# Retention and GELU MLP on one core: block 1's state, scores and outputs moved forward, masks built later

## The chip, the cores and the metric

The kernel runs on 1 core of one Trainium2 chip. The metric is the device time of one execution in microseconds (us). Before the change it is 288.76 us, the median of 3 runs (288.71 to 288.97).

In the profile the engines are PE (TensorE, matrix products), PEld (its weight loads), DVE (VectorE), ACT (ScalarE), POOL (GpSimd) and SP (SyncE, which here only issues DMA transfers; its queue is shown as SPq). L419 is line 419 of the kernel before.

## The reference

Retention over 8 batches and 8 heads, 576 positions, head size 64, then a two-layer MLP with a tanh GELU over the 4608 tokens.

```python
def _attn_ref(q, k, v):
    scores = scale * np.matmul(q, k.transpose(0, 1, 3, 2))
    gamma = 1.0 - 2.0 ** (-5.0 - np.arange(H, dtype=np.float32))
    rel = pos[:, None] - pos[None, :]
    Dmat = np.where(rel >= 0, gamma[:, None, None] ** rel[None, :, :], 0.0)
    return np.matmul(scores * Dmat[None, :, :, :], v)

def _moe_ref(x, w_in, w_out):          # x: 4608 x 512, d_ff: 2048
    h = x @ w_in
    g = 0.5 * h * (1.0 + np.tanh(c * (h + 0.044715 * h * h * h)))
    return g @ w_out
```

All inputs and the output are float32.

## The kernel before

The retention is done in chunks. Each batch has four chunks of 128 positions and a tail of 64; the tails of all batches make a ninth block of tokens. Within a chunk, scores are masked and multiplied with the values; what came before a chunk enters through a state (keys times values), which is carried from half chunk to half chunk by a decay. So a batch b goes through these steps, each of them a helper:

- `load` and `cc` (cast): the chunks of k, q and v come in as float32 by DMA issued on SP, into a ring of 16 buffers (`ld`). POOL, ACT or DVE casts them to float16 and scales k and q by powers of the decay (L294 for k, L275 for q, L271 on POOL or L269 on ACT for v). `pump` issues the next load for each buffer that a cast frees.
- `turn_dma` (L324): two DMA transposes on SP bring the cast k and q into `tt`, with the head dimension on partitions. Batches 0 and 1 are turned by PE instead.
- `scores`: 64 matmuls of 64x64 (L419, `st <- tt`) into four PSUM banks, then `masks` (L444, DVE): four multiplications with the causal mask `cm`, which give `ret` and release the banks. `masks(b, 0)` handles the first two chunks and `masks(b, 1)` the last two.
- `state` (L419, `us <- cv, ck`): 32 matmuls of 64x64 for two chunks, into two PSUM banks. `scan_halves` on DVE (L494, L477, L472) adds them up with the decay `gx` and, between the operations, has ACT cast the running state to float16 (L497); `spread` casts the state behind the chunk (L505). `later(b, c)` is a scan and a spread.
- `outs(b, g)`: first the contributions of the states to two chunks (`xs <- tt, tbb`), then, between two tiny matmuls called `turn`, the `state` of what comes next, then the contributions of the states that are read from the other half of the partitions and of the masked scores (`xs <- ret, cv`); about 90 to 98 small matmuls with the state among them. `put` then casts `xs` into `xT`, the MLP's input, on ACT (one of them on DVE).

The MLP works on blocks of 512 tokens (t = 0 to 8). Layer one multiplies xT with w_in, and ACT applies the GELU into `gT` (L605 and L612 in halves for t = 0 and 1, L584 and L590 for the others). `act_sums` (L746 to L750, DVE) forms sums of gT for a seven-product scheme, by which layer two (`prod`, L769) needs seven block products of 256 columns instead of eight; `after` adds the products up on DVE and ACT (L783, L822, L839) and stores them in two halves, `send` (L786), by DMA on SP.

The order of all work is written out by hand. Block t is a list of steps, numbered 0 to 29 here: 0 to 15 are layer one (in block 1 eight matmuls of 256 columns each, from block 2 on four matmuls of 512 columns for each), 16 to 29 the fourteen pieces of layer two (m, u) in the order m = 1, 6, 5, 7, 2, 4, 3, eight matmuls each. `at(t, u, f)` puts the retention work f of the next batch behind step u of block t, and `run` calls it there. Every engine executes its instructions in that order, and waits only for what it reads or for a buffer that it overwrites. So block 1 computes batch 1's MLP while batch 2's retention is prepared, and block t prepares batch t + 1.

The eight PSUM banks are handed out by `bank` from a queue, the longest released first, and given back by `drop`.

Around the change, in block 1 before:

- step 0: POOL builds the masks `cm` and `tm` (`chunk_masks`, L218 and L220) and the decays `gx` (`decays_turned`, L232), between its casts of batch 1 and those of batch 2.
- end of block 0: `after(0, 4, ...)` issues the store of the second half of block 0's output on SP, behind the loads of batch 2's values up to there.
- steps 0 to 10: the casts of batch 2, and at step 5 its two transposes on SP.
- step 12: the loads of batch 3 may be issued (`resume`); step 16: POOL waits at `gate` (L1077), a copy of one column of the last sum of gT, before it casts batch 3.
- step 16: `state(2, 0)`; steps 17 and 18: `later(2, 0)` and `later(2, 1)`; step 19: `scores(2)` with both masks; step 25: `outs(2, 0)` with `state(2, 1)`, and `later(2, 2)`; step 26: `later(2, 3)`; step 28: `outs(2, 1)` with `state(3, 0)`.

In the blocks 2, 3 and 4 the scores of the next batch stand behind step 10, in the later ones behind step 9.

Of the kernel before, what the change touches and what calls it, by code (L numbers as in the profile page):

```python
# [20 lines left out]
def kernel(  # L21
# [9 lines left out]
    nc = tc.nc  # L31
# [19 lines left out]
    gam = [1.0 - 2.0 ** (-5.0 - h) for h in range(H)]  # L51
# [129 lines left out]
    for n in range(2):  # L181
# [3 lines left out]
            out=lp[:, 32 + 16 * n : 48 + 16 * n].rearrange("p (x h) -> p x h", h=8),  # L185
# [12 lines left out]
    tbb = [const.tile([128, 2 * NC - 1, HP, 64], F16, name=f"tbb{i}") for i in range(2)]  # L198
# [17 lines left out]
    def chunk_masks():  # L216
        for m, pattern in ((cm, [[1, 2], [2, 32]]), (tm, [[1, 64]])):
            nc.gpsimd.memset(m, 1.0)  # L218
            for r, base in ((128, 64), (64, 0)):
                nc.gpsimd.affine_select(  # L220
                    out=m[0:r], in_=m[0:r], compare_op=ALU.is_ge, fill=0.0, base=base, pattern=pattern, channel_multiplier=-1
                )
# [6 lines left out]
    def decays_turned():  # L229
        for h in range(H):  # L230
            u = 64 * (h % 2 ^ h // 4)
            nc.gpsimd.memset(gx[u : u + 64, h // 2, :], gam[h] ** 128)  # L232

    tbt = [const.tile([128, HP, 64], F16, name=f"tbt{i}") for i in range(NT4)]

# [204 lines left out]
    def masks(b, g):  # L440
        n = 8 if b < PAIR else 4
        for r, t in enumerate(att[b].pop(("st", g))):
            m = sb.tile([128, 512], F16, tag="ret", name="ret", bufs=6)
            nc.vector.tensor_tensor(  # L444
                out=m[:, 0 : 64 * n].rearrange("p (n i) -> p n i", n=n), in0=t[:, 0 : 64 * n].rearrange("p (n i) -> p n i", n=n),
                in1=(cm if b < PAIR else tm).unsqueeze(1).to_broadcast([128, n, 64]), op=ALU.mult,
            )
            drop(t)
            att[b]["ret"][g, r] = m
# [35 lines left out]
        if last:  # L485
            drop(us)

    def scan_halves(b, c):
        a = att[b]
        us, o = a.pop(("U", c))  # L490
        u, v = (t[:, 256 * o : 256 * o + 256].rearrange("p (q d) -> p q d", d=64) for t in us)
        if c == 0:
            t = sb.tile([128, HP, 64], F32, tag="ts", name="ts", bufs=2)
            nc.vector.tensor_copy(out=t, in_=u)  # L494
        else:
            t = plus(u, a["w"], "ts")
        nc.scalar.copy(out=tbb[b % 2][:, 2 * c], in_=t)  # L497
        times(a, c, plus(v, t, "vs"), gx)
        if o == 1:
            drop(us[0]), drop(us[1])  # L500
# [275 lines left out]
    def after(t, m, u):  # L776
        last = t == NTB - 1
        if u == 0 and not (last and m == 3 or t in WIN and m == 4) or u == 1 and t in WIN and m == 4:
            return
        def pr(tag):  # L780
            return op[tag].rearrange("p (u d) -> p u d", u=2)
        def add(o, a, b):
            nc.vector.tensor_tensor(out=o, in0=a, in1=b, op=ALU.add)  # L783
        def send(o, i):
            if t < B:
                nc.sync.dma_start(  # L786
                    out=out[S * t : S * t + TB, :].rearrange("(u i p) d -> p u i d", u=2, i=2)[:, :, i, :], in_=o
                )
                return
            both(o, i, slice(0, HD))  # L790
        def both(o, i, d):
            rows = out.rearrange("(b s) d -> b s d", s=S)
            for h, e in enumerate((nc.sync, nc.scalar)):
                r = rows[2 * i + h :: 4, M0 : M0 + TL, d]
                e.dma_start(out=r.rearrange("v s d -> s v d"), in_=o[TL * h : TL * h + TL, :, d])
        def end(o, i, v, d=slice(0, DM)):
            b = 4 * v + 2 * i
            for h, e in enumerate((nc.sync, nc.scalar)):
                r0 = S * (b + h) + M0
                e.dma_start(out=out[r0 : r0 + TL, d], in_=o[TL * h : TL * h + TL, d])  # L800
        if t == 0 and m != 1 and m != 2:
            if m == 6:
                for n, a, b in (("u2", "s1", "B"), ("u3", "u2", "C")):
                    keep[n] = sb.tile([128, 2, HD], F32, tag="k" + n[1], name="k" + n[1], bufs=1)
                    add(keep[n], keep[a], pr(b))
                    drop(op.pop(b))
                add(keep["o0"][:, :, HD:DM], keep["u3"], pr("E"))
                drop(op.pop("E"))
                send(keep["o0"], 0)
            elif m == 7:  # L810
                keep["o1"] = ost()
                add(keep["o1"][:, :, HD:DM], keep["u3"], pr("D"))
                add(keep["u2"], keep["u2"], pr("D"))
                drop(op.pop("D"))
            elif m == 4:
                add(keep["o1"][:, :, 0:HD], keep["u2"], pr("F"))
                drop(op.pop("F"))
                send(keep["o1"], 1)
            return
        if m == 1:  # L820
            keep["s1"] = sb.tile([128, 2, HD], F32, tag="k1", name="k1", bufs=1)
            nc.scalar.copy(out=keep["s1"], in_=pr("A"))  # L822
        elif m == 6:
            keep["u2"] = sb.tile([128, 2, HD], F32, tag="k2", name="k2", bufs=1)
            add(keep["u2"], keep["s1"], pr("B"))
            for f in range(0, NH if t in WIN else 0, 2):
                act_sums(t, f, f + 2, parts=(1,))
        elif m == 7:
            keep["u3"] = sb.tile([128, 2, HD], F32, tag="k3", name="k3", bufs=1)
            add(keep["u3"], keep["s1"], pr("B"))  # L830
            keep["o1"] = ost()
            add(keep["o1"][:, :, HD:DM], keep["u3"], pr("C"))
            if last:
                both(keep["o1"], 1, slice(HD, DM))
            drop(op.pop("B")) if t in WIN else None
            drop(op.pop("C")) if t in WIN else None
        elif m == 2:
            keep["o0"] = ost()
            nc.scalar.copy(out=keep["o0"][:, :, 0:HD], in_=pr("A"))  # L839
            drop(op.pop("A"))  # L840
            if last:
                both(keep["o0"], 0, slice(0, HD))
        elif m == 5 and t in WIN:
            add(keep["u2"], keep["u2"], pr("C"))
        elif m == 3 and last:
            add(keep["o0"][:, u, HD:DM], keep["u2"][:, u], pr("EF"[u])[:, u])
            end(keep["o0"][:, u], 0, u, slice(HD, DM))
        elif m == 3:
            x = "E" if t in WIN else "C"
            add(keep["o0"][:, :, HD:DM], keep["u2"], pr(x))  # L850
            drop(op.pop(x))
            send(keep["o0"], 0)
        elif m == 4 and t in WIN:
            add(keep["o1"][:, :, 0:HD], keep["u3"], pr("D"))
            drop(op.pop("D"))
            send(keep["o1"], 1)
        elif m == 4:
            add(keep["o1"][:, :, 0:HD], keep["s1"], pr("B"))
            drop(op.pop("B"))
            send(keep["o1"], 1)  # L860
# [27 lines left out]
    def later(b, c):  # L888
        (scan if b < NPE else scan_halves)(b, c)
        spread(b, c, A.copy)  # L890
# [53 lines left out]
    def at(t, u, f, last=False):  # L944
        events.setdefault((t, u, last), []).append(f)
# [60 lines left out]
    group(1, 0, ((0, 8), (0, 10)), (0, 10), (0, 12), late=(1, 1))  # L1006
    casts2(1, 1, (0, 10), (0, 10), P)
    group(1, 1, ((0, 13), (1, 0)), (1, 2), (1, 5), late=(1, 6))
    at(1, 0, lambda: (chunk_masks(), decays_turned()))

    at(6, 0, lambda: load_tails(TP[7]))
    at(6, 18, lambda: cast_tails(TP[7]))
# [5 lines left out]
    for t, b in TP.items():  # L1018
        at(t, 3, lambda b=b: tail_values(b))

    def scores(b, tails=None):
        w = [score(b, g) for g in range(2)] if b < B else []
        if tails is not None:
            w.append(score(PAIR + tails, 0))
        pack(w)
        if b < B:
            masks(b, 0), masks(b, 1)
        if tails is not None:
            masks(PAIR + tails, 0)

# [13 lines left out]
        for x in todo:  # L1044
            put(*x)

    U2 = (19, 25, 28)
    at(1, 16, lambda: pack([state(2, 0)]))
    for c in range(2):
        at(1, 17 + c, lambda c=c: later(2, c))  # L1050
    for t in range(1, B):
        b, tl = t + 1, TP.get(t)
        s0, o0, o1 = U2 if t == 1 else (10 if t in (2, 3, 4) else 9, 15, 24)
        at(t, s0, lambda b=b, tl=tl: scores(b, tl))
        at(t, o0, lambda b=b, tl=tl: outs(b, 0, tl, (b, 1) if b < B else None))
        if b == B:
            continue
        at(t, 25 if t == 1 else 16, lambda b=b: later(b, 2))
        at(t, 26 if t == 1 else 20, lambda b=b: later(b, 3))
        at(t, o1, lambda b=b: outs(b, 1, None, (b + 1, 0) if b + 1 < B else None))  # L1060
        if b + 1 < B:
            for c in range(2):
                at(t + 1, c, lambda c=c, nb=b + 1: later(nb, c))
# [119 lines left out]
```

## Time and profile before

| what | value |
| --- | --- |
| median of 3 runs | 288.76 us (288.71 to 288.97) |
| the profiled execution, its own time | 288.71 us |
| its span in the profile | 287.0 us |
| granted TensorE clock over the span | 1.0 |
| HBM read, written | 36.70 MB, 9.44 MB |
| L584 PE MATMUL, 352 of 128x512 | 79.0 us busy, 379 ns mean |
| L605 PE MATMUL, 256 of 128x256 | 29.9 us busy, 273 ns mean |
| block 1, layer one | 51.1 to 67.8 us |
| block 1, layer two | 67.8 to 84.7 us |
| blocks 2, 3, 4 | 84.7 to 114.0, to 143.4, to 172.8 us |

The time of one execution is a little longer than the span, which runs from the first to the last recorded instruction. Busy time on PE counts each matmul from its start to its modelled end, and neighbours overlap; a mean of 273 ns for 256 columns does not mean that one starts every 273 ns (they start 109 ns apart). A number in brackets behind an instruction of the timeline is the engine's idle time before it, and the name behind the arrow what ended it; "issue" is written where the profile shows nothing that the engine waited for. In a line of stretches each engine has its busy time and the count of its instructions, then come the granted clock, the share of time in which the 16 DMA engines were busy, and GB/s.

### The profile page before, as it was taken

Reading aid. Unit: us, or ns where it says so; the run is one execution under the profiler, and the core shown is the slowest. Engines: PE = TensorE matmul, PEld = TensorE weight load, DVE = VectorE, ACT = ScalarE, POOL = GpSimd, SP = SyncE. Lnnn points to the kernel's source line nnn. Section 1 sums busy time; section 2 is a strip of 40 time slices with the busy share of each in tenths; the row PEclk is TensorE's granted clock in tenths of the full one; section 3 lists DMA queues with packets and bytes.
Section 4 is the critical chain, followed back from the end, with each engine's and each line's share of the span. In section 5 each row is a group of like instructions: output and inputs, shape, how many; then the busy total and the mean of one; then the engine's idle time right before and its main releaser. Section 6 shows DMA issues by size and latency. Waiting matters only on the chain.

```text
span 287.0 us, 9420 instructions
## 1 busy us (share of the span) xinstructions
PE 274.5 (96%) x3986; PEld 202.1 (70%) x3986; DVE 196.5 (68%) x412; ACT 169.3 (59%) x326; POOL 115.3 (40%) x225
## 2 busy tenths in 40 slices
PE   6889998999989999999999999999999999999993
PEld 3558876888864588458844884488448887887782
DVE  6785988686866664577368636763687767875863
ACT  5477655996248563866386746574666358407800
POOL 5579859980692089007910670059230000000000
PEclk9999999999999999999999999999999999999999
DMA  7999999989989999999799859997972030012013
GB/s 200 304 380 339 386 295 260 254 217 188 234 186 221 247 218 182 248 226 230 167 218 267 203 127 241 243 225 126 254 162 39 2 148 1 2 47 103 0 39 110
DMA packets 127306, 54.09 MB, mean 188 GB/s; under 512 B 93472, under 2 KB 119072, under 8 KB 127264
## 3 DMA queue, kind: packets, MB, share of 16 engines
q1 hardware_dynamic: 126672, 52.97, 76.5%
q8 instruction: 31, 0.51, 0.8%
q10 hardware_dynamic: 592, 0.52, 0.6%
q14 instruction: 11, 0.09, 0.1%
HBM read 36.70 MB, written 9.44 MB: 161 GB/s over the span
## 4 chain that ended last, share of the span: by engine, by line
PE 81%; DMA 9%; DVE 3%; POOL 3%; issue 1%; ACT 1%; SPq 0%; POOLq 0%; DVEq 0%
PE hp L584 26%; PE opB L769 13%; PE opA L769 10%; PE opC L769 9%; PE hp L605 5%; DMA ld<-in_moe_w_in_dram 4%; PE hB L678 3%; PE xs L419 3%; DMA ld<-in_q_dram 3%; DMA ld<-in_moe_w_out_dram 2%; PE hC L678 2%; PE st L419 2%; POOL cq L283 1%; PE us L419 1%; PE opD L769 1%; PE tr L312 1%
## 5 line engine op out<-in xcount | busy, mean ns | idle before, releaser
L584 PE MATMUL hp<-xT,w_in_sb 128*128 128x512 f16 x352 | 79.0, 379 | 0.0
L590 ACT ACTIVATE gT<-hp 128x512 f16<-128x512 f32 x88 | 50.8, 598 | 29.6 <-PE hp L584 29.1
L769 PEld LDWEIGHTS <-gT 128*128 128x128 f16 x576 | 55.0, 98 | 8.7 <-issue 1.2
L584 PEld LDWEIGHTS <-w_in_sb 128*128 128x128 f16 x352 | 34.0, 98 | 37.9 <-DVE xT L570 0.2
L769 PEld LDWEIGHTS <-s 128*128 128x128 f16 x432 | 42.0, 98 | 4.9
L769 PE MATMUL opA<-w_out_sb,gT 128*128 128x256 f16 x288 | 36.2, 273 | 0.7 <-ACT w_out_sb L875 0.5
L294 POOL TENSOR_TENSOR ck<-ld,sc 128x128 f16<-128x128 f32 (+1 forms) x72 | 33.5, 491 | 4.2 <-DMA ld<-in_k_dram 4.2
L746 DVE TENSOR_TENSOR s<-gT 128x512 f16<-128x512 f16 x36 | 16.1, 448 | 26.2 <-ACT gT L590 19.6
L605 PE MATMUL hp<-xT,w_in_sb 128*128 128x256 f16 x256 | 29.9, 273 | 1.1 <-POOL w_in_sb L875 0.7
L275 POOL TENSOR_TENSOR cq<-ld,sc 128x256 f16<-128x256 f32 x48 | 29.8, 639 | 0.0
L1077 POOL COPY gate<-s 128x1 f16<-128x1 f16 x5 | 0.9, 190 | 71.5 <-DVE s L750 71.5
L605 PEld LDWEIGHTS <-w_in_sb 128*128 128x128 f16 x256 | 24.3, 98 | 5.5 <-POOL w_in_sb L875 2.5
L769 PE MATMUL opB<-wt,gT 128*128 128x256 f16 x224 | 26.8, 273 | 0.0
L570 ACT CAST xT<-xs 128x512 f16<-128x512 f32 x23 | 15.4, 735 | 13.1 <-PE xs L419 13.1
L783 DVE TENSOR_TENSOR k<-k,opB 128x512 f32<-128x512 f32 x17 | 11.7, 686 | 13.4 <-PE opB L769 11.5
L612 ACT ACTIVATE gT<-hp 128x512 f16<-128x512 f32 x32 | 18.5, 603 | 3.8 <-PE hp L605 3.5
L747 DVE TENSOR_TENSOR s<-s,gT 128x512 f16<-128x512 f16 x36 | 16.8, 468 | 1.2
L769 PE MATMUL opB<-wt,s 128*128 128x256 f16 x144 | 17.4, 273 | 0.0
L769 PE MATMUL opC<-wt,s 128*128 128x256 f16 x144 | 17.2, 273 | 0.0
L748 DVE TENSOR_TENSOR gT<-gT 128x512 f16<-128x512 f16 x36 | 16.7, 463 | 0.0
L444 DVE TENSOR_TENSOR ret<-st,cm 128x512 f16<-128x512 f32 x24 | 14.9, 683 | 2.4 <-PE st L419 2.4
L750 DVE TENSOR_TENSOR s<-gT,s 128x512 f16<-128x512 f16 x36 | 16.0, 457 | 0.0
(135 smaller groups left out, 429.1 us busy)
## 6 DMA issues: line engine op xcount, KB each, us to landing
ld<-in_q_dram SPq DMA_DIRECT2D x32, 256.0 KB, 5.5
ld<-in_k_dram SPq DMA_DIRECT2D x32, 256.0 KB, 5.6
ld<-in_v_dram SPq DMA_DIRECT2D x32, 256.0 KB, 5.3
out_dram<-ost SPq DMA_DIRECT2D x16, 512.0 KB, 4.0
ld<-in_moe_w_in_dram SPq DMA_DIRECT2D x16, 256.0 KB, 5.7
ld<-in_moe_w_out_dram SPq DMA_DIRECT2D x16, 256.0 KB, 5.8
lt<-in_k_dram SPq DMA_DIRECT2D x8, 128.0 KB, 5.0
lt<-in_q_dram SPq DMA_DIRECT2D x8, 128.0 KB, 4.2
```

The costliest lines, as they stand in the source:

```text
L275: eng.tensor_tensor(out=a[key][:, 1024 * g + 512 * x : 1024 * g + 512 * x + 512].rearrange("p (n l d) -> p l n d", l=2, d=D)[:, y ^ x], in ...
L294: eng.tensor_tensor(out=dh[:, o], in0=x, in1=sc[:, s0, i].unsqueeze(2).to_broadcast(list(x.shape)), op=ALU.mult)
L419: nc.tensor.matmul(out, lhsT, rhs, start=k not in opened, stop=True, skip_group_check=True)
L584: nc.tensor.matmul(hp.rearrange("p (g t) -> p g t", t=TL), w_in_sb[:, ct, 128 * fc : 128 * fc + 128], xT[:, o : o + TB // TL, ct, :], star ...
L590: nc.scalar.activation(out=gT[t][:, fc].rearrange("p i n -> p (i n)"), in_=hp, func=AF.Gelu_apprx_tanh)
L605: nc.tensor.matmul(hps[n][:, 256 * x : 256 * x + 256].rearrange("p (g t) -> p g t", t=TL), w_in_sb[:, ct, 128 * (fs[n] + x) : 128 * (fs[n] ...
L612: nc.scalar.activation(out=gT[t][:, f : f + 2, 2 * u : 2 * u + 2, :].rearrange("p f i n -> p f (i n)"), in_=hp.rearrange("p (f n) -> p f n ...
L746: nc.vector.tensor_tensor(out=s["1"], in0=a21, in1=a22, op=ALU.add)
L747: nc.vector.tensor_tensor(out=s["2"], in0=s["1"], in1=a11, op=ALU.subtract)
L748: nc.vector.tensor_tensor(out=a21, in0=a11, in1=a21, op=ALU.subtract)
L750: nc.vector.tensor_tensor(out=s["4"], in0=a12, in1=s["2"], op=ALU.subtract)
L769: nc.tensor.matmul(op[tag][:, HD * u : HD * u + HD], lhs(f), rhs[:, f], start=(new and f == 0), stop=(f == NH - 1), skip_group_check=True,)
```

## The change

- `decays_turned` sets `gx` on DVE (`nc.vector.memset`) instead of POOL; it stays behind step 0 of block 1.
- `chunk_masks` moves from step 0 to step 11 of block 1, and so, on POOL, behind the casts of batch 2.
- The store of the second half of block 0's output is issued at step 6 of block 1. On SP it then stands behind the two transposes of batch 2 instead of ahead of them.
- `state(2, 0)` moves from step 16 to step 12, into layer one. Both its scans run behind step 14, on DVE ahead of the last `act_sums` of block 1 (`scan_halves` gets a parameter `then`, by which the cast of the running state on ACT is issued later, at steps 16 and 17). The spreads stay at 17 and 18.
- `scores(2)` moves from step 19 to 17; `masks(2, 0)` follows there, `masks(2, 1)` at step 19.
- `outs(2, 0)` moves from step 25 to 22, with `later(2, 2)` at 22 and `later(2, 3)` at 24. `outs(2, 1)` stays at 28.
- In blocks 2, 3 and 4 the scores move from step 10 to step 9.

No matmul or weight load of PE is added or removed (7,972; with branches and waits of their own the program has 7,990 PE instructions before and 7,992 after); DVE gains the eight memsets that POOL loses.

```diff
     def decays_turned():
         for h in range(H):
             u = 64 * (h % 2 ^ h // 4)
-            nc.gpsimd.memset(gx[u : u + 64, h // 2, :], gam[h] ** 128)
+            nc.vector.memset(gx[u : u + 64, h // 2, :], gam[h] ** 128)
...
-    def scan_halves(b, c):
+    def scan_halves(b, c, then=lambda f: f()):
...
-        nc.scalar.copy(out=tbb[b % 2][:, 2 * c], in_=t)
+        then(lambda: nc.scalar.copy(out=tbb[b % 2][:, 2 * c], in_=t))
         times(a, c, plus(v, t, "vs"), gx)
...
             elif m == 4:
                 add(keep["o1"][:, :, 0:HD], keep["u2"], pr("F"))
                 drop(op.pop("F"))
-                send(keep["o1"], 1)
+                at(1, 6, lambda o=keep["o1"]: send(o, 1))
...
-    at(1, 0, lambda: (chunk_masks(), decays_turned()))
+    at(1, 0, decays_turned)
+    at(1, 11, chunk_masks)
...
-    def scores(b, tails=None):
+    def scores(b, tails=None, wait=None):
...
         if b < B:
-            masks(b, 0), masks(b, 1)
+            masks(b, 0)
+            at(*wait, lambda: masks(b, 1)) if wait else masks(b, 1)
...
-    U2 = (19, 25, 28)
-    at(1, 16, lambda: pack([state(2, 0)]))
+    U2 = (17, 22, 28)
+    at(1, 12, lambda: pack([state(2, 0)]))
     for c in range(2):
-        at(1, 17 + c, lambda c=c: later(2, c))
+        at(1, 14, lambda c=c: scan_halves(2, c, lambda f, c=c: at(1, 16 + c, f)))
+        at(1, 17 + c, lambda c=c: spread(2, c, A.copy))
     for t in range(1, B):
         b, tl = t + 1, TP.get(t)
-        s0, o0, o1 = U2 if t == 1 else (10 if t in (2, 3, 4) else 9, 15, 24)
-        at(t, s0, lambda b=b, tl=tl: scores(b, tl))
+        s0, o0, o1 = U2 if t == 1 else (9, 15, 24)
+        at(t, s0, lambda b=b, tl=tl, w=(1, 19) if t == 1 else None: scores(b, tl, w))
...
-        at(t, 25 if t == 1 else 16, lambda b=b: later(b, 2))
-        at(t, 26 if t == 1 else 20, lambda b=b: later(b, 3))
+        at(t, 22 if t == 1 else 16, lambda b=b: later(b, 2))
+        at(t, 24 if t == 1 else 20, lambda b=b: later(b, 3))
```

## The prediction

> **What bounds the kernel now.** I read the page first, then the stretches by stage, the waits of PE, and the timelines of PE, SP and DVE around block 1.
>
> ```profile
> span 287.0 us, 9420 instructions
> PE 274.5 (96%) x3986; PEld 202.1 (70%) x3986; DVE 196.5 (68%) x412; ACT 169.3 (59%) x326; POOL 115.3 (40%) x225
> ...
> q8 instruction: 31, 0.51, 0.8%
> ```
>
> PE is busy 96% of the span, so a change pays only where PE stands still. The q8 line, needed below, is a DMA queue with 31 packets of 0.51 MB: 16,384 bytes each, 258 for each of PE's 7,990 instructions in the built program, so one packet is 256 instructions of 64 bytes.
>
> ```profile
> core 0: us, PE busy (x) PEld busy (x) DVE busy (x) ACT busy (x) POOL busy (x), PEclk, DMA share, GB/s
> 67.80:84.70 16.90, 15.82 (x398) 13.41 (x395) 12.58 (x26) 6.62 (x14) 9.99 (x20) 1.00 1.03 215
> 84.70:114.00 29.30, 29.30 (x432) 19.70 (x431) 17.45 (x38) 17.75 (x34) 14.78 (x31) 1.00 0.95 211
> ```
>
> The change sits in layer one (51.1 to 67.8 us, PE busy 16.70 of 16.70) and layer two (67.8 to 84.7) of block 1, and moves one step in blocks 2 to 4. Of all this only the first line has idle PE: 16.90 less 15.82 is 1.08 us. The waits of PE give that as one piece, and the timeline shows where:
>
> ```profile
> PE xs L419 <- issue: 1.1, 1, 1.1
> ```
> ```profile
> 81.49 0.32 PE L419 MATMUL xs<-tt,tbb 64*64 64x64 f16 x16
> ...
> 82.07 0.44 PE L419 MATMUL xs<-ret,cv 64*64 64x64 f16 x25
> 83.58 0.25 PE L419 MATMUL xs<-ret,cv 64*64 64x64 f16 x7 [1.08 <-issue]
> ```
>
> PE stops between two matmuls of one kind, 25 done and 7 to go, and no producer is named: the masks `ret` ended at 75.85, the value casts at 65.7, the state casts at 81.02. From the last start, 82.31, to the next, 83.58, is 1.27 us where 0.01 is usual: 1.26 us lost. I read it as PE out of instructions. It stops after its 1,245th matmul; with the few others that is instruction 2,496 of the program, and 256 earlier is matmul 1,117. The DMA records have a q8 packet starting at 81.02, and one at 84.69, just after PE goes on. So a packet seems to be asked for when PE enters the block before: matmul 1,117 ran at 78.50, the packet began 2.52 us later among loads that fill the queues (DMA share 1.03), and its instructions ran 2.56 us after that, 5.08 us in all. PE used up its block in 3.81 us, because it held 104 small matmuls (64x64, some 0.01 us apiece) and only 24 wide ones (0.109 us). Counting boundaries every 256 instructions through the run, the others had 2.62 us or more after the packet's start and show no stop.
>
> **The change part by part.** *Masks and decays.* POOL's L218 to L232 run from 49.84 to 52.65, 2.81 us ahead of block 2's casts. These now start 2.81 us earlier: the last key cast ends at 62.38 - 2.81 = 59.57, the last query cast at 60.90; the last query load landed at 57.60, so no load delays them. The masks (1.49 us) follow until 62.4, under the 6.44 us for which POOL waited at L1077. The eight memsets of gx on DVE go by those of gt (L227): 112 ns each, 8 in 1.26 us; DVE idles from 52.26 to 54.86, so nothing. Without that cover it is 1.26 us on the L363 masks, which end at 58.37 with their readers at 58.38.
>
> *Turned copies ahead of the store.*
>
> ```profile
> 61.17 0.86 SPq L786 DMA_DIRECT2D out_dram<-ost  x1
> 62.40 3.68 SPq L324 DMA_TRANSPOSE tt<-ck  x1
> 66.18 3.08 SPq L324 DMA_TRANSPOSE tt<-cq  x1
> ...
> 85.76 1.84 SPq L324 DMA_TRANSPOSE tt<-ck  x1
> 87.69 2.20 SPq L324 DMA_TRANSPOSE tt<-cq  x1
> ```
>
> On SP the first pair waited for the key cast (62.38) and ran behind a 512 KB store; it landed at 71.10, 0.67 before the scores. Now both casts are done when the last value load is issued (61.08), so it starts there. By its own 8.70 us it lands at 69.8, by the 6.75 us of the pair at 85.76 (no store ahead) at 67.9. The scores, two steps earlier but behind the state, start at 71.77 less two steps of 0.873 us, 70.0: no wait, 0.2 us to spare at worst. At the old landing they would wait 1.1 us: this part only pays for the next. The store waits behind the pair until about 65; its buffer is wanted at 76.86. Behind it stand block 3's loads: before, they began at 69.31, now some 2 us sooner.
>
> *First state in layer one.* The 32 matmuls of `state(2, 0)` (68.66 to 69.04) run unchanged, after step 12 (about 65.1). The casts of its values end at 63.22. PE's work is the same, the switch is 96 ns behind L605 as behind L769: zero. On DVE the six scan operations (70.00 to 72.77, 2.8 us) now stand ahead of the last four sums of block 1.
>
> ```profile
> 67.39 0.42 DVE L750 TENSOR_TENSOR s<-gT,s 128x512 f16<-128x512 f16 x1
> 68.53 0.43 DVE L746 TENSOR_TENSOR s<-gT 128x512 f16<-128x512 f16 x1 [0.72 <-ACT gT L612]
> ```
>
> DVE is free at 67.7; scan to 70.5; the four sums (1.47 us) to 72.0, where they made way at 70.0. The product that reads them (L769 opB, u = 1) starts at 71.6, but needs their second result from its fifth matmul, 72.0; that is there at 71.4. The POOL gate L1077 moves from 70.15 to about 72.1; the first cast behind it ran at 73.57, on a load. Zero.
>
> *Scores, split masks, outputs.* PE: first outputs at 77.78 less three steps, 75.16, and their `us` matmuls 0.09 later (77.87 before), 75.25. DVE: two masks 72.0 to 73.2 (0.6 apiece), a sum to 73.8, two masks, the last from 74.4 to 75.05. In the first outputs `us` takes the two banks that these last masks release (eight banks are then held, so no other is free): 0.2 to spare. Here is the new tight wait. If the four sums ran at the pace of the group at 59.24 (2.88 us beside a busy POOL), PE would wait 1.2 us; POOL is idle then, so I take 0 and keep 0 to 0.5.
>
> *Scores at step 9 in blocks 2 to 4.* One step of four 512-wide matmuls is 0.87 us. In block 2 the turned copies landed at 92.51 for scores at 94.30; in 3 and 4 1.35 us or more would be left. With the step and the gain below the scores come at 92.2, and the copies, whose loads start about 2 us and casts 1.3 us sooner, land at about 91.2. Zero, with 0 to 0.3 if they do not move.
>
> *The stop itself.* The first outputs now hold matmuls 1,016 to 1,106, so the block from 1,117 to 1,245 holds 37 wide matmuls in place of 24, and the second outputs come behind 48 wide ones. PE needs 37 x 0.109 + 0.20 (switch) + 0.82 (81.49 to 82.31) = 5.06 us for it, where 5.08 were needed. And it is entered among wide matmuls, where the packet lagged less: -0.1, 1.1, 1.1, 0.0 at the boundaries at 67.4, 83.6, 96.1, 102.9, at most 1.87 (56.6). So the 1.26 us goes. Bound: with the largest lag of the run, 2.98 (at 153.2), 0.48 comes back. A bound below: no other idle exists here, so no more than 1.26 can be won. The neighbouring blocks take 5.5 us or more by the same count.
>
> **Sum.** The profiled execution took 288.71 us (span 287.0 and 1.7 around it), 0.05 below the median. 288.71 - 1.26 + 0 = 287.45, with a little for the tight waits 287.5. PE has no other gap until 225 us, so the gain reaches the end.
>
> **Rivals.** *The stop half returns*: lag as at 153.2, 287.45 + 0.48, with slight waits 288.0. For: queues are as full as before. Against: the lags in wide stretches.
>
> *The stop belongs to the outputs, not to the supply*, and moves with them: 288.7. For it: the page names no cause, and packets of 16 KB pass 30 other boundaries freely. Against: the count of 256, and the packet that begins before and never after. [...]
>
> *Late copies in block 2, slower*: place, the gate L1077. It waits for sums that now stand behind the scan; if these run slowly and POOL's casts start d later than 73.57, the copies land at 92.51 + d and PE waits 0.34 + d. From d = 0.92 the kernel is slower than before; a DVE group at the 2.88 us pace and loads that come no sooner than now give d = 1.4: 287.45 + 1.74 = 289.2. For: 0.9 us of cover are given away by the step from 10 to 9. Against: 1.3 us of slack at the gate, and loads that start sooner.
>
> **How the numbers follow.** The forecast (287.5) 0.58, the half return 0.10, the stop that stays 0.17, late copies 0.15. What can be told from no change is about 0.2%, 0.58 us: below 288.18 is faster (0.68), 288.7 the same (0.17), 289.2 slower (0.15). The likeliest case alone spans 287.3 to 288.0. The range, 287.2 to 288.9, takes in the first three and leaves out the last.
>
> **What would show it.** Right: PE's wait xs <- issue is gone, PE busy within 0.2 us of the stretch in block 1's layer two, the copies of block 2 land before 69.9, the packet for matmul 1,245 starts 2.5 us or more ahead. Wrong: PE waiting at us L419 for DVE ret L444, at st L419 for a DMA of tt in blocks 1 to 4, or another stop by "issue" in the middle of small matmuls.

## The result and the profile after

| | before | changed |
| --- | --- | --- |
| median of 8 runs on the same chips | 289.01 us (287.77 to 289.28) | 287.54 us (286.54 to 288.51) |
| ratio to before, 95% interval | | 0.9952 (0.9930 to 0.9973) |
| profiled execution, its span | 288.71, 287.0 us | 288.51, 286.8 us |

The kernel is faster by 0.5% (0.3 to 0.7%), 1.4 us. The two profiled executions differ by only 0.2 us (the changed kernel's was the slowest of its eight), and a reader who looks at the spans alone would find nothing. So the stage has to be read. From the stretches of the changed kernel (us, busy time and count of PE, PEld, DVE, ACT, POOL, then clock, DMA share and GB/s):

```profile
51.10:68.10 17.00, 17.00 (x279) 14.86 (x277) 11.18 (x30) 15.34 (x31) 12.07 (x27) 1.00 1.02 221
68.10:84.18 16.08, 15.76 (x371) 13.52 (x368) 12.93 (x27) 6.85 (x16) 8.95 (x19) 1.00 0.99 231
84.18:113.50 29.32, 29.32 (x431) 19.66 (x431) 17.31 (x38) 17.92 (x34) 14.79 (x31) 1.00 1.03 219
```

PE's idle time in layer two of block 1 fell from 1.08 to 0.32 us. The waits of PE say that what is left is another wait:

```profile
PE st L419 <- DMA tt<-cq: 0.3, 1, 0.3
```

and its timeline in the second outputs shows that the stop is gone, all 32 matmuls of `xs <- ret, cv` in one piece:

```profile
82.19 0.32 PE L419 MATMUL xs<-tt,tbb 64*64 64x64 f16 x16
...
82.77 0.50 PE L419 MATMUL xs<-ret,cv 64*64 64x64 f16 x32
83.20 1.05 PE L769 MATMUL opC<-w_out_sb,s 128*128 128x256 f16 x8
```

By the start times of the matmuls, three parts of the span can be told apart: up to block 1 (51.15 us before, 51.47 after, though nothing in the change acts there), block 1 from the last turning matmul ahead of it to the first matmul of block 2 (33.54, then 32.71), and from there to the last matmul (197.50, then 197.75). The change is worth 0.83 us in its own stage in this execution; the other two parts took 0.57 us more, which hides most of it. In fourteen profiled executions the first part ended between 50.5 and 52.7 us and the third mostly took 197.5 to 198.0. That is why single times of one kernel lie 2 us apart, and why the experiments are read by block 1's own length first, one profiled execution each, and by ratios second. The profiled execution of e1_count96 was disturbed by one DVE operation (last section), so that its block 1 is not listed.

### The profile page after: what moved, and what is told of

Read it like the earlier page. It is cut to its first block, busy times and chain, and to the rows that moved or that the text cites. A ratio compares the mean times of both kernels' runs of the same rounds, so it can differ in the third digit from the quotient of the medians.

```text
span 286.8 us, 9420 instructions
## 1 busy us (share of the span) xinstructions
PE 274.3 (96%) x3986; PEld 201.8 (70%) x3986; DVE 195.9 (68%) x420; ACT 169.4 (59%) x326; POOL 113.7 (40%) x217
## 4 chain that ended last, share of the span: by engine, by line
PE 74%; DMA 10%; POOL 7%; SPq 4%; DVE 2%; issue 1%; ACT 0%; POOLq 0%
PE hp L584 26%; PE opB L769 13%; PE opA L769 9%; PE opC L769 9%; PE hB L678 3%; PE xs L419 3%; SPq L96 3%; DMA ld<-in_k_dram 2%; DMA ld<-in_moe_w_in_dram 2%; POOL ck L294 2%; DMA ld<-in_q_dram 2%; DMA ld<-in_moe_w_out_dram 2%; POOL cq L275 2%; PE hp L605 2%; DMA tt<-cq 2%; PE st L419 2%
## 5 line engine op out<-in xcount | busy, mean ns | idle before, releaser
L269 ACT CAST cv<-ld 128x512 f16<-128x512 f32 x24 | 14.7, 622 | 6.8 <-DMA ld<-in_v_dram 6.1
L748 DVE TENSOR_TENSOR gT<-gT 128x512 f16<-128x512 f16 x36 | 16.1, 446 | 0.0
```

Source lines behind the costliest of these rows:

```text
L748: nc.vector.tensor_tensor(out=a21, in0=a11, in1=a21, op=ALU.subtract)
```

## The experiments

All times are compared with the kernel before on the same chip. The table gathers them; "stop" is PE's idle time by "issue" in the second outputs over the usual 0.01 us, "copy" when the turned queries of batch 2 landed, counted from the start of block 1, "st wait" the gap ahead of the scores over the usual 0.20.

| run | block 1, us | stop | copy | st wait | ratio to before (95%) |
| --- | --- | --- | --- | --- | --- |
| before | 33.54 | 1.26 | 19.95 | 0 | |
| changed | 32.71 | 0 | 19.12 | 0.39 | 0.9952 (0.9930 to 0.9973) |
| e1_count96 | not listed | 0 | 17.21 | 0 | 0.9974 (0.9951 to 0.9997) |
| e10_count96 | 32.32 | 0 | 17.70 | 0 | 0.9978 (0.9959 to 0.9997) |
| e2_count40 | 33.21 | 0.91 | 18.69 | 0 | 1.0017 (0.9995 to 1.0039) |
| e3_outs25 | 33.69 | 1.40 | 16.99 | 0 | 1.0013 (0.9984 to 1.0042) |
| e6_only_outs | 32.88 | 0 | 19.68 | 0 | 1.0008 (0.9984 to 1.0032) |
| e5_after_again | 32.53 | 0 | 18.96 | 0.22 | 0.9974 (0.9954 to 0.9994) |
| e4_scores18 | 32.33 | 0 | 16.53 | 0 | 0.9973 (0.9949 to 0.9997) |
| e8_scores18 | 32.33 | 0 | 16.74 | 0 | 0.9972 (0.9952 to 0.9992) |
| e7_undo_pool | 32.55 | 0 | 18.98 | 0.24 | 0.9983 (0.9965 to 1.0002) |
| e11_undo_pool | 33.38 | 0 | 19.80 | 1.07 | one run |
| e12_store_ahead | 32.69 | 0 | 19.11 | 0.37 | one run |
| e9_step10 | 32.33 | 0 | 18.68 | 0 | 1.0004 (0.9972 to 1.0036) |

**Is the stop the instructions' own?** Nothing of block 1 is touched in the next two; only the count of instructions ahead of it changes.

```diff
+    def tiny(n):
+        t = ps.tile([128, 512], F32, tag=f"p{spare[0]}", name="tiny", bufs=1)
+        for _ in range(n):
+            nc.tensor.matmul(t[0:64, 0:4], ident[0:64, 0:64], ident[0:64, 0:4], start=True, stop=True)
...
     filler(6)
+    tiny(32)
...
+    tiny(32)
     up_halves(0, 0, (0, 2))
...
+    at(0, -10, lambda: tiny(32))
```

> The kernel before, with 96 matmuls of 64x64 by 4 columns added early (32 each at about 11.5, 16 and 21 us, where PE waits for loads anyway; their results are never read). Nothing around block 1 is changed but the count of PE's instructions ahead of it. Theory (PE runs out of instructions at a boundary of 256): the block that ends in the second outputs then starts among the first outputs' wide neighbours and holds about 38 wide matmuls, so the stop of 1.26 us in block 1 is gone and the time is 1.0 to 1.3 us below the kernel before. Rival (the stop belongs to the outputs or to their data): it stays, with the same 7 matmuls left, and the time is that of the kernel before within 0.3 us.

> The kernel before with 96 small matmuls added early, once more, for a profile with an undisturbed clock. Theory: no stop by issue in block 1, which takes 32.2 to 32.4 us from its first matmul to that of block 2, where the kernel before took 33.5. Rival: 33.5.

Measured: no stop, and 0.22 to 0.26% less time from 96 matmuls more. That is 0.6 to 0.75 us, less than the 1.0 to 1.3 us expected of the first, though both intervals (from 0.1 to 1.2 or 1.4 us) reach into it. The stage is read from the second profile. Its timeline of PE:

```profile
81.19 0.32 PE L424 MATMUL xs<-tt,tbb 64*64 64x64 f16 x16
...
81.76 0.50 PE L424 MATMUL xs<-ret,cv 64*64 64x64 f16 x32
82.19 1.05 PE L774 MATMUL opC<-w_out_sb,s 128*128 128x256 f16 x8
```

Block 1 takes 32.32 us, 1.22 less than before, with its order of work unchanged. The rival, a stop that belongs to the outputs or their data, is out. The 40 of the other run are placed likewise (20 and 20):

> The same with 40 small matmuls added early (20 at about 11.5 and 20 at 16 us). Theory (instructions): the boundary comes 40 matmuls earlier in the outputs, and the block still holds only 24 wide ones, so the stop stays at 1.0 to 1.4 us but with 47 small matmuls of the second outputs left in place of 7; the time is that of the kernel before within 0.3 us. Rival (data): the stop stays with 7 left.

Measured, in the timeline of PE:

```profile
83.37 0.19 PE L424 MATMUL xs<-tt,tbb 64*64 64x64 f16 x1
84.30 0.32 PE L424 MATMUL xs<-tt,tbb 64*64 64x64 f16 x15 [0.73 <-issue]
84.42 0.44 PE L424 MATMUL xs<-ret,cv 64*64 64x64 f16 x32
```

The stop is there with 15 and 32 left, 47, as the count says and no data could: it again follows matmul 1,245, counted with the forty. It cost 0.91 us, a little less than expected: its packet began sooner (1.65 us after the boundary before, not 2.52), but its instructions ran later behind it (3.14 us, not 2.56). The run has a second stop, of 0.86 us behind matmul 2,012, one short of six boundaries further on, in the middle of wide matmuls of block 3 that had never waited. Of the 128 matmuls ahead of it 110 were 64x64, and PE had run through them in 3.05 us:

```profile
132.75 0.38 PE L774 MATMUL opB<-wt,s 128*128 128x256 f16 x2
133.83 0.39 PE L774 MATMUL opB<-wt,s 128*128 128x256 f16 x2 [0.70 <-issue]
```

**Which part of the change removed it?** First the changed kernel with the outputs alone put back:

```diff
-    U2 = (17, 22, 28)
+    U2 = (17, 25, 28)
...
-        at(t, 22 if t == 1 else 16, lambda b=b: later(b, 2))
-        at(t, 24 if t == 1 else 20, lambda b=b: later(b, 3))
+        at(t, 25 if t == 1 else 16, lambda b=b: later(b, 2))
+        at(t, 26 if t == 1 else 20, lambda b=b: later(b, 3))
```

> The changed kernel with one part undone: the first outputs of batch 2 back behind step 25, their scans at 25 and 26; state, scores, split masks, mask building and store stay changed. Theory (instructions): the 24 wide matmuls between the two outputs are back, and so is the stop of 1.0 to 1.4 us with 7 matmuls left; with the wait of the scores for the turned copies the time is 0 to 0.4 us above the kernel before. Rival (the state in layer one or the earlier masks removed the stop): no stop, and 1.0 us or more below the kernel before.

```profile
82.02 0.43 PE L419 MATMUL xs<-ret,cv 64*64 64x64 f16 x24
83.67 0.26 PE L419 MATMUL xs<-ret,cv 64*64 64x64 f16 x8 [1.22 <-issue]
```

The stop is back, 1.40 us with 8 left (one matmul earlier, presumably because the changed program has two PE instructions more), and block 1 takes 33.69. State, masks and store forward are worth nothing without the outputs. Then the kernel before with the outputs alone moved (`U2 = (19, 22, 28)`, scans at 22 and 24):

> The kernel before with one part of the change alone: the first outputs of batch 2 behind step 22 in place of 25, their scans at 22 and 24. Theory (24 more wide matmuls between the two outputs end the stop; the other parts only pay for the earlier place): no stop by issue, but the state in the first outputs waits about 0.6 us at us L419 for the last masks (DVE ret L444, which ended at 75.85 where PE comes at 75.25); time 0.4 to 0.9 us below the kernel before and 0.4 to 0.8 above the changed kernel. Rival (the other parts carry the gain): within 0.3 us of the kernel before.

Its waits of PE:

```profile
PE us L419 <- DVE ret L444: 0.4, 1, 0.4
```

No stop, and in its place the wait for the last masks, 0.55 us by the start times. Block 1 takes 32.88, 0.66 less than before: what the other parts pay for is those 0.55 us. The time does not show the 0.66 us: 1.0008 (0.9984 to 1.0032) is 0.2 us above the kernel before, where 0.4 to 0.9 below was expected, and the interval reaches 0.5 below. By time alone the rival, within 0.3 us of the kernel before, stands, and the run decides nothing; in its profile the rest of the span took 0.4 us longer. The case against the rival rests on block 1 alone.

**What are the masks behind the casts and the store behind the copies worth?**

```diff
-                at(1, 6, lambda o=keep["o1"]: send(o, 1))
+                send(keep["o1"], 1)
...
-            nc.vector.memset(gx[u : u + 64, h // 2, :], gam[h] ** 128)
+            nc.gpsimd.memset(gx[u : u + 64, h // 2, :], gam[h] ** 128)
...
-    at(1, 0, decays_turned)
-    at(1, 11, chunk_masks)
+    at(1, 0, lambda: (chunk_masks(), decays_turned()))
```

> The changed kernel with masks and decays built on POOL at step 0 again, and the store ahead of the turned copies. Theory: the copies land near 71.1 again while the scores come at 70.0, a wait of 0.6 to 1.5 us at st L419 for a DMA of tt; no stop by issue; time 0.5 to 1.4 us above the changed kernel. Rival (the copies are paced by the loads, not by POOL and the store): a wait under 0.3 us and the time of the changed kernel.

> Masks and decays on POOL at step 0 and the store ahead of the copies, a second look. The query copy landed 19.0 us after block 1's first matmul in the look before, as in two looks at the changed kernel (19.1 and 19.0), and 16.5 to 17.0 in three others with POOL and store changed. If the parts matter, it lands at 18.5 or later again and never at 17; if the loads alone set it, it can land at 17.

The first profile gave a wait of 0.24 us and a time 0.3 us above the changed kernel's: a miss, and what the rival said. The second gave

```profile
PE st L419 <- DMA tt<-cq: 1.0, 1, 1.0
```

and block 1 at 33.38, the gain all but gone. With the store alone ahead again (the first of the three edits):

> The changed kernel with the store alone ahead of the turned copies again (masks stay behind the casts). If the store costs the copies what its issue and its 512 KB take, the query copy lands 1 to 2.5 us later than 16.5 to 17.0 after block 1's first matmul, 18 to 19.5, and the scores wait 0 to 0.6 us; if POOL's casts decide, 17.

it landed at 19.11, a wait of 0.37. The table forbids a simple answer. With either the store or both ahead in the changed kernel the copy landed 19.0 to 19.8 us into block 1 in three profiles of three. With both parts as changed it landed at 16.5 to 17.0 in three (e3, e4, e8), but at 18.7 to 19.1 in three more (changed, e5, e9). And in e10, which is the kernel before with both parts ahead, it landed at 17.70, so an early landing does not need the parts either.

The start of the pair separates more clearly. As changed, SP began it right behind the last value load, 8.7 to 10.9 us into block 1 in six profiles. With the masks ahead of the casts it began right behind the last key cast, at 10.8 to 11.4 in six (before, e2, e6, e7, e10, e11), and with the store alone ahead right behind that, at 9.8. From there to the landing the pair took 7.7 to 8.7 us as changed and 6.9 to 9.3 otherwise. So the parts let the pair start earlier; that the store slows the pair itself is not shown, and what sets those 7 to 9 us was not isolated.

**Steps 10 and 9 in blocks 2 to 4.** `(10 if t in (2, 3, 4) else 9, 15, 24)` again:

> The changed kernel with one part undone: scores behind step 10 again in blocks 2, 3 and 4. Theory: PE has no gap there in either order, so block 1 takes 32.3 to 32.8 us from its first matmul to that of block 2 as in the changed kernel, and the time is that of the changed kernel within 0.3 us. Rival (step 9 comes too early for the turned copies and costs some of the gain): the tile switch ahead of the scores in block 2 is shorter by 0.05 us or more in each of blocks 2 to 4.

Block 1 is as short as in the best of these runs, 32.33. In block 2 the switch ahead of the scores is 0.05 us shorter than in the changed kernel (0.31 us from start to start, not 0.36), in 3 and 4 it is the same: the rival's sign shows in block 2 alone. The time (1.0004, 0.9972 to 1.0036) is not that of the changed kernel within 0.3 us, as was expected, but the interval is too wide to tell; this execution entered block 1 at 52.69.

The profile shows one thing more. In block 3 PE lost 0.23 us behind matmul 1,883, in the first outputs, with the packet only 2.81 us ahead. This is a boundary of the same count: 1,245 + 5 x 128 = 1,885, less two, presumably for instructions that only wait. e6, also with step 10, lost 0.15 us behind matmul 1,884. With step 9 four wide matmuls lie inside that block of instructions, 0.87 us more, and the changed kernel shows no loss there although its packet lagged as much (3.0 us). So step 9 seems to have a use that the prediction did not count.

**A version beyond both.** The changed kernel with `U2 = (18, 22, 28)`: the scores one step later.

> The changed kernel with the scores of batch 2 behind step 18 in place of 17. Theory: the scores come 0.87 us later, the turned copies are there (the wait of 0.39 us at st L419 is gone), the masks on DVE are no later since DVE is busy with the sums until then, and the time is 0.3 to 0.5 us below the changed kernel, 1.5 to 1.9 below the kernel before. Rival (the wait only moves): the first outputs now wait for the last masks at us L419 by 0.3 us or more and the time is that of the changed kernel.

> The changed kernel with the scores behind step 18 once more, now beside the changed kernel on one chip. No wait at st L419 and none at us L419; 0 to 0.5 us below the changed kernel, according to whether that waits for its copies.

No wait at st or us in either profile, and block 1 at 32.33 twice, 0.2 to 0.4 below the changed kernel's 32.53 and 32.71 in its two profiles. That is as short as the 32.32 of e10, where no gap is left. The times beside the changed kernel on one chip, 0.9972 and 0.9974, can't tell the two apart, so the 0.3 to 0.5 us expected of e4 is not shown by time.

## Why the prediction was right

*The stop is a lack of instructions, 1.26 us:* shown by e1, e2, e3 and e10, as above. In the changed kernel the packet for matmul 1,245 began 4.8 us ahead, where 2.5 or more was asked for, and 3.5 to 5.2 us ahead in the eight other profiles with the outputs at step 22. That a packet is asked for when PE enters the block before stays a reading: in the kernel before, packets began between 2.0 us ahead of that moment and 3.0 us behind it. That one packet holds 256 of PE's instructions, 128 matmuls with their weight loads, was an estimate from 31 packets for 7,990 instructions; the two stops of e2 stand 767 matmuls apart, six times 128 less one. In the kernel before, PE's waits name "issue" once, 1.1 us at this boundary, whose block held 104 matmuls of 64x64; e10, in which only the count is shifted, won 1.22 us in block 1.

*37 wide matmuls instead of 24 end it, 5.06 us against 5.08 needed:* right, and mostly by the second of its two reasons. The block took 5.06 us (77.95 to 83.01), which by itself would have been 0.02 too short; the lag was 0.23 us in the wide stretch, not 2.5. In the eight other profiles with the outputs at 22 it was -0.2 to 1.5 us, and the half return occurred in none.

*The copies land between 67.9 and 69.8, no wait:* the one term that was clearly mis-sized. They landed at 70.59, and PE waited 0.39 us (0.22 in e5). Two signs of being right failed with it (the landing before 69.9, PE busy within 0.2 us of the stretch, where 0.32 was idle), and one sign of being wrong appeared: the wait at st L419 in block 1. I had put the longer time of the pair before, 8.70 us, down to the store ahead and taken 6.75 from the clean pair. SP's timeline of the changed kernel:

```profile
62.40 3.16 SPq L324 DMA_TRANSPOSE tt<-ck  x1
65.66 2.82 SPq L324 DMA_TRANSPOSE tt<-cq  x1
68.58 0.54 SPq L786 DMA_DIRECT2D out_dram<-ost  x1
```

With no store ahead the pair still took 8.19 us, and it started at 62.40 and not at 61.1, since the value loads were issued later in this execution (from 55.59 to 62.30, not 54.87 to 61.08). POOL's first key cast for batch 2 came at 51.46, not 49.84, after waits of 0.65 and 0.36 us for key loads, and the last key cast ended at 60.89, not 59.57. The clean pair had no loads ahead of it either (0 GB/s from 85.50 to 86.38 in the kernel before), which may be why it was short; that was not tried. Both ends of my range took the loads' start from one execution, which moves by more than the 0.2 us that I had to spare.

*The tight wait for the last masks, 0.2 us to spare:* right in kind. In the changed kernel the last mask ended at 75.92 (75.05 forecast) and the state's matmuls came at 75.97, late themselves by the 0.39; e6 shows the wait with the other parts taken away, 0.55 where about 0.6 was expected.

*Scores at step 9 in blocks 2 to 4:* the copies that the scores in block 2 read landed at 92.83, not at about 91.2, and later than the 92.51 before. PE waited 0.05 us for them (0.05 in e5 too); the price of zero held only nearly.

*Masks, gx on DVE, the state in layer one, the gate:* nothing of them shows in PE's time. The gate moved from 70.15 to 72.99 (72.1 expected) and the first cast behind it from 73.57 to 73.64.

*Sum:* 288.71 - 1.26 + 0 was forecast. In the stage it was 1.26 won and 0.39 given back at the scores, with some 0.04 in smaller pieces: 0.83. The median of 287.54 agrees with 287.5 better than this sum deserves, and that part is luck: e5, the same kernel again, was 0.75 us (0.2 to 1.3) faster than the kernel before, not 1.4.

## What to carry to other kernels

Where a saturated PE stands still by "issue" in the middle of like instructions, count instructions. The five stops of over 0.2 us in these runs came at the end of blocks of 128 matmuls of which 104 to 110 were 64x64. PE ran through them in 3.05 to 5.52 us, their packet began 1.35 to 2.96 us after PE had entered the block, and the instructions ran 2.56 to 3.14 us after that. A short block alone is not enough: near 140 us a block with 98 small matmuls took 4.3 to 4.5 us in eleven profiles and never stopped PE, because its packet began at most 0.65 us after PE had entered it. What sets that lag was not isolated.

Putting wide matmuls between dense small ones, or merely shifting the count by 96 small matmuls at places where PE waited, removed the stop of 1.26 us here; any edit ahead shifts the count too, and can move the stop somewhere else, as e2 shows (0.86 us behind matmul 2,012). A cover of 0.2 us that rests on when DMA loads were issued in one execution is no cover: the last value load was issued by 62.30 us in the changed kernel, where 61.08 had been taken from the kernel before.

## What the runs showed of the hardware that was not expected

The profiled execution of e1_count96 (295.64 us; the eleven others took 287.4 to 288.4) shows one DVE operation of 128x256 float32 take 6.36 us, which took 0.45 to 0.83 us in the thirteen other profiles. It ended when POOL, which had cast without a pause, had done its last cast:

```profile
55.84 6.36 DVE L477 TENSOR_TENSOR ws<-vs,gt 128x256 f32<-128x256 f32 x1
62.12 0.68 DVE L368 TENSOR_TENSOR ret<-st,pm 128x512 f16<-128x512 f32 x1
```
```profile
57.02 1.32 POOL L299 TENSOR_TENSOR ck<-ld,sc 128x256 f16<-128x256 f32 x3
58.30 1.18 POOL L280 TENSOR_TENSOR cq<-ld,sc 128x256 f16<-128x256 f32 x2
59.45 1.32 POOL L299 TENSOR_TENSOR ck<-ld,sc 128x256 f16<-128x256 f32 x3
60.73 1.18 POOL L280 TENSOR_TENSOR cq<-ld,sc 128x256 f16<-128x256 f32 x2
```

POOL ended at 61.91, and DVE's next operation began at 62.12. PE waited 4.3 us for the masks behind it. After that the granted clock was 0.50 from 62.80 to 65.40 and 0.52 to 68.90, and matmuls of 256 columns started 0.213 us apart where 0.109 is usual. The same POOL casts ran in every profile; that they held the operation is not shown, and why it was held once was not tried.

From the start of a packet of instructions to the first of them on PE it took 2.56, 2.67, 2.73, 2.81 and 3.14 us in the five stops of over 0.2 us, for packets that themselves took 1.2 to 1.8.
